# Gated linear attention ahead of two expert layers: units of 256 tokens, with neighbouring decays multiplied before the transposes

## The chip, the cores and the metric

One core of a Trainium2 chip runs the whole program as one launch. The metric is device microseconds of an execution, as the median of the runs shown; times come from the hardware profiler's records of one more execution.

## The reference

The program is a gated linear attention followed by two feed-forward layers, in float32. Only the first part is touched by the change.

```
q,k,v,f_logit: [4 batches, 8 heads, 768 tokens, 48]
f = 1/(1+exp(-f_logit))
for t in range(768):                    # per batch and head
    state = f[t][:,None]*state + outer(k[t], v[t])      # 48 x 48
    y[t] = q[t] @ state
x = y as [3072 tokens, 384]
# then: 8 experts of 384 tokens each, filled in the order of the gate's logits:
#       relu(x @ w1[e]) @ w2[e]       (384 -> 1024 -> 384)
# then: h = x @ w_in; (h*clip(h+3,0,6)/6) @ w_out       (384 -> 2048 -> 384)
```

## The kernel before

`attention` works through the 3,072 tokens in chunks of C=128 (24 chunks, index j). Inside a chunk the recurrence is a masked matrix product; from chunk to chunk a state of 48 x 48 a head is carried. The decays enter as running products: q is multiplied by P, the product of the decays from the chunk's start up to its token (prefix), k by S, the running product taken from the chunk's end and started from the reciprocal of the whole (suffix).

What a chunk needs of q, k and f is prepared in units of U=384 tokens (three chunks, 8 units, index u). Raw f, k and q of a unit are loaded with three consecutive tokens a partition (runs of 3·48 floats, 576 bytes; `load`, L60), v with one token a partition (192 bytes, L64). `reorder` (L66 to L70) moves one of the three tokens at a time into a padded layout: tanh for f on ScalarE (`pmf`), a copy for k on ScalarE (`pmk`), a copy for q on GpSimd (`pmq`). `tgroup` (L72) handles one pair of heads p and one of f, k, q: three transposes (L85) into a PSUM tile of the pool pT (five banks), so that channels are on partitions and 384 tokens lie along the row; for f an ACT pass makes f=0.5·tanh+0.5 (`ff`, L89; two buffers), VectorE runs the prefix scan (L97), takes the product at each chunk's end, held above 2^-60 (L99), its reciprocal (L100), and the suffix scan (L95). For k and q, VectorE multiplies the transposed tile by S (`kh`, L102) or P (`qt`, L109). Unit 0 goes through the same ahead of the loop, by halves of the heads, with q's multiply on GpSimd (L107). The order of the twelve groups of a unit is the list ORD; `group` puts the VectorE operations of one group behind the transposes of the next.

The loop over j (L271 to L305) does, in each turn, in this order: group; `l_mm` for chunk j-1 (L218: output projected into place and gate logits; eviction `y` on ScalarE, store to x_dram); group; `ya_mm` (L142: q times state of chunk j; L136: the 128 x 128 scores of chunk j+1 into banks pA0 and pA1); their evictions `am` on ScalarE (L168) with masking on GpSimd (L169); `y_mm` (L193: masked scores times v; eviction `yt`); `kv_mm` (L204: turned keys times v, into bank pA0) whose result updates the state on VectorE and GpSimd (L209, L211, L212); group; `kt_mm` (L176: keys of chunk j+1 turned back, eviction `kt`); group. Three turns prepare one unit ahead.

In the gaps runs `prep`, a list of steps that fetches float64 weights w_in (twelve blocks of 512 KB) and half of w_out (eight of 384 KB) and converts them on VectorE, ScalarE and GpSimd (L922 to L959, L719, L720). PREP says at which groups a step is taken. All loads and stores are issued by SP in program order. PSUM has eight banks: five for pT, pA0, pA1, and one (`pC`) which holds the constant operand of the prefix scan and the floor 2^-60.

After the loop come the routing of tokens to experts and 8 experts with both feed-forward layers.

Of the kernel before, what the change touches and what calls it, by code (L numbers as in the profile page):

```python
# [14 lines left out]
C=128; U=384; NP=4; NU=B*S//U; NCH=B*S//C  # L15
PMIN=2.0**-60; PB=5

def attention(tc, q,k,v,f,wg, x_dram, lg, ident, pmin, ranges, prep, setup, spin):
    nc=tc.nc
    ctx=ExitStack()  # L20
    with ctx:
# [21 lines left out]
        for i in range(2):  # L43
            t=cs.tile([128,3,H,64],F32,name=f"v{i}"); nc.gpsimd.memset(t[:,:,:,D:],0.0); VP.append(t)
# [4 lines left out]
        for i in range(2):  # L49
            s=cs.tile([128,NP,64],F32,name=f"St{i}"); nc.vector.memset(s[:,:,D:],0.0); St.append(s)  # L50
        FF=[]
        for i in range(2):
            t=cs.tile([128,U+1],F32,name=f"ff{i}"); nc.vector.memset(t[:,U:],1.0); FF.append(t)
        raw={}
        def load(u,nm,h0=0,h1=H):
            b,hf=divmod(u,2)
            if nm!='v':
                src={'f':f,'k':k,'q':q}[nm]
                t=ld.tile([128,H,3*D],F32,name=nm+"r",bufs=1) if h0==0 else raw[nm,u]
                nc.sync.dma_start(t[:,h0:h1],bass.AP(tensor=src.tensor,offset=src.offset+b*H*S*D+h0*S*D+hf*U*D,ap=[[3*D,128],[S*D,h1-h0],[1,3*D]]))  # L60
# [5 lines left out]
        def reorder(u,nm,r,h0=0,h1=H):  # L66
            x=raw[nm,u].rearrange("p h (r d) -> p h r d",d=D)[:,h0:h1,r]; o=perm[nm].rearrange("p r a s d -> p (a s) r d")[:,h0:h1,r,:48]
            if nm=='f': nc.scalar.activation(o,x,AF.Tanh,scale=0.5)
            elif nm=='k': nc.scalar.copy(o,x)
            else: nc.gpsimd.tensor_scalar(o,x,1.0,0.0,op0=OP.mult,op1=OP.add)  # L70
        KH={};QT={};PC={};PP={};SS={};SF={}
        def tgroup(u,p,nm):  # L72
            if p==0 and nm=='f':
                PC[u]=pmin[:,u]
            if p==0 and nm=='k':
                KH[u]=KHB[u%2]
            if p==0 and nm=='q':
                t=wk.tile([128,NP,U],F32,name="qt"); QT[u]=t
            if u==0:
                n=ORD.index((p,nm))%4  # L80
                pt=ps.tile([128,C*3],F32,name=("pT","pA0","pT","pA1")[n],bufs=PB if n%2==0 else 1).rearrange("p (c r) -> p c r",r=3)
            else: pt=ps.tile([128,C,3],F32,name="pT",bufs=PB)
            x=perm[nm]
            for r in range(3):
                nc.tensor.transpose(pt[:,:,r],x[:,r,p].rearrange("p a d -> p (a d)"),ident)  # L85
            pf=pt.rearrange("p c r -> p (c r)")
            if nm=='f':
                ff=FF[p%2]
                nc.scalar.activation(ff[:,:U],pf,AF.Identity,bias=half[:,0:1],scale=0.5)  # L89
                if p%2==0: PP[u,p//2]=wk.tile([128,2,U],F32,name="P")  # L90
                P2=PP[u,p//2]; P=P2[:,p%2]; pp=slice(p-1,p+1)
                V=nc.vector; ends=lambda t: t.rearrange("p a (c t) -> p a c t",t=C)[:,:,:,C-1]
                def suffix():
                    SS[u,p]=wk.tile([128,U],F32,name="S",bufs=3)
                    V.tensor_tensor_scan(SS[u,p][:,::-1],ff[:,1:U+1][:,::-1],m1[:,p%2,::-1],1.0,op0=OP.mult,op1=OP.max)  # L95
                SF[u,p]=suffix
                ops=[lambda: V.tensor_tensor_scan(P,m0,ff[:,:U],1.0,op0=OP.max,op1=OP.mult)]  # L97
                if p%2==0: return ops,[]
                return (ops+[lambda: V.tensor_tensor(out=PC[u][:,pp],in0=ends(P2),in1=least,op=OP.max)],  # L99
                        [lambda: V.reciprocal(ends(m1),PC[u][:,pp]),SF[u,p-1]])  # L100
            elif nm=='k':
                return [lambda: nc.vector.tensor_mul(KH[u][:,p],pf,SS[u,p])],[]  # L102
            else:
                if u==0:
                    t=wk.tile([128,2,NP,C],F32,name="am").rearrange("p s a c -> p (s a c)")[:,:U]
                    nc.scalar.copy(t,pf)
                    nc.gpsimd.tensor_tensor(out=QT[u][:,p],in0=t,in1=PP[u,p//2][:,p%2],op=OP.mult)  # L107
                def whole_q():
                    if u>0: nc.vector.tensor_mul(QT[u][:,p],pf,PP[u,p//2][:,p%2])  # L109
                return [whole_q],([] if p%2 else [SF[u,p+1]])  # L110
        prev=([],[]); rest=[]; late=[]
        def group(new,fill=None,flush=False):

            nonlocal prev,rest
            a=list(rest); b=list(prev[0]); ops=[]
            while a or b:
                if a: ops.append(a.pop(0))
                if b: ops.append(b.pop(0))
            for i,op in enumerate(ops):
                op()  # L120
                if i==0 and fill: fill(); fill=None
            while late: late.pop(0)()
            if fill: fill()
            rest=prev[1]; prev=new
            if flush:
                for op in prev[0]: op()
                prev=([],prev[1])
        AM={};KT={};pA={}
        def a_mm(j):
            u,c=divmod(j,3)  # L130
            pA[j]=[]
            for s in range(2):
                t=ps.tile([128,NP,C],F32,name=f"pA{s}"); pA[j].append(t)
            def quarter(p,s,h):
                r=slice(64*s,64*s+64); k=c*C+64*h
                nc.tensor.matmul(pA[j][s][64*h:64*h+64,p],KH[u][r,p,k:k+64],QT[u][r,p,c*C:(c+1)*C],start=True,stop=True)  # L136
            return quarter
        def s_mm(j):
            u,c=divmod(j,3)
# [30 lines left out]
        def kt_mm(j):  # L170
            u,c=divmod(j,3)
# [25 lines left out]
        def kv_mm(j):  # L197
            u,c=divmod(j,3); first=j%6==0
# [27 lines left out]
        ORD=[(0,'f'),(1,'f'),(0,'q'),(0,'k'),(2,'f'),(3,'f'),(1,'q'),(1,'k'),(2,'q'),(2,'k'),(3,'q'),(3,'k')]  # L226
# [5 lines left out]
        def reorder0(h,nms='fkq'):  # L232
            for nm in nms:
                for r in range(3): reorder(0,nm,r,h,h+4)
        reorder0(0,'fq')
        for nm in 'fkq': load(1,nm)
        WARM=(4,1,8,0); RF,RK=2,4
# [5 lines left out]
        for i,(p,nm) in enumerate(ORD):  # L243
            if i==RF: reorder0(0,'k'); reorder0(4,'f')
            if i==RK: reorder0(4,'q')
            if i==RK+2: reorder0(4,'k')
            group(tgroup(0,p,nm),flush=(p,nm)==ORD[-1])
            warm(WARM[3] if i<2 else WARM[1] if i<11 else WARM[2])
        later=[]
        def refill(u,nm):  # L250
            if u<NU:
                if nm in 'fk':
                    for r in range(3): byact.append(lambda r=r: reorder(u,nm,r))
                    if u+1<NU: byact.append(lambda: later.append(lambda: load(u+1,nm)))
                    return
                for r in range(3): reorder(u,nm,r)
                if u+1<NU: later.append(lambda: load(u+1,nm))
        byact=[]
        def one():

            if byact: byact.pop(0)()
            if len(byact)==1: byact.pop(0)()
        refill(1,'f')
        while byact: one()
        for nm in 'kq': refill(1,nm)
        one(); one()
# [3 lines left out]
        PREP=((0,2),(0,),(0,1,2))  # L270
        for j in range(-1,NCH+1):  # L271
            tu,ti=divmod(j+1,3)
            tu+=1
            g=[(tu,)+x for x in ORD[4*ti:4*ti+4]] if tu<NU else [None]*4
            if j>=0 and j%3==0 and j//3+1<NU: load(j//3+1,'v')
            def take(j,i):
                for _ in range(int(i in PREP[ti]) if j<20 else 2): next(prep,None)
            def tg(i):
# [4 lines left out]
            if ti!=1: one()  # L283
# [853 lines left out]
```

## Time and profile before

| | |
|---|---|
| median of three runs | 845.35 us (845.16 to 845.64) |
| the profiled execution | 842.33 us |
| its span, first to last instruction | 840.5 us |
| busy: TensorE, VectorE, ScalarE, GpSimd | 796.7, 560.4, 366.2, 141.3 us |
| mean granted TensorE clock | 0.988 of full speed |

Attention takes about the first 170 us of the span, the experts the rest from about 195 us on. The busy shares over the whole span are those of the experts, which keep TensorE full; what the change touches has to be read in the first 170 us alone. PE is TensorE's matmuls, PEld its weight loads, DVE VectorE, ACT ScalarE, POOL GpSimd, SP the engine that issues the transfers.

### The profile page before, as it was taken

Reading aid. Unit: us, or ns where it says so; the run is one execution under the profiler, and the core shown is the slowest. Engines: PE = TensorE matmul, PEld = TensorE weight load, DVE = VectorE, ACT = ScalarE, POOL = GpSimd, SP = SyncE. Lnnn points to the kernel's source line nnn. Section 1 sums busy time; section 2 is a strip of 40 time slices with the busy share of each in tenths; the row PEclk is TensorE's granted clock in tenths of the full one; section 3 lists DMA queues with packets and bytes.
Section 4 is the critical chain, followed back from the end, with each engine's and each line's share of the span. In section 5 each row is a group of like instructions: output and inputs, shape, how many; then the busy total and the mean of one; then the engine's idle time right before and its main releaser. Section 6 shows DMA issues by size and latency. Waiting matters only on the chain.

```text
span 840.5 us, 16833 instructions
## 1 busy us (share of the span) xinstructions
PE 796.7 (95%) x6447; PEld 762.4 (91%) x6447; DVE 560.4 (67%) x1526; ACT 366.2 (44%) x759; POOL 141.3 (17%) x233
## 2 busy tenths in 40 slices
PE   7898999888999999999999999999999999999994
PEld 6777788777989899899999999999999999999994
DVE  7999999778688548745964776666757523642431
ACT  5666776514345325423541454154316423541431
POOL 4665653311001101010100101100300020010001
PEclk9999999969999999999999999999999999999998
DMA  8899994173013112211422232322222321321000
GB/s 222 233 244 236 221 232 128 64 244 97 1 37 114 57 39 76 85 39 57 141 72 94 67 97 91 101 66 86 89 81 85 94 85 57 115 93 45 3 1 33
DMA packets 86554, 84.56 MB, mean 101 GB/s; under 512 B 30272, under 2 KB 74432, under 8 KB 86464
## 3 DMA queue, kind: packets, MB, share of 16 engines
q1 hardware_dynamic: 83392, 73.96, 31.1%
q0 software_dynamic: 3072, 9.44, 3.5%
q8 instruction: 52, 0.85, 0.4%
q14 instruction: 38, 0.31, 0.1%
HBM read 73.94 MB, written 9.44 MB: 99 GB/s over the span
## 4 chain that ended last, share of the span: by engine, by line
PE 64%; DVE 15%; issue 12%; ACT 5%; DMA 2%; POOL 2%; SPq 0%; POOLq 0%; ACTq 0%; DVEq 0%
PE acc L723 9%; PE pF L723 9%; PE acc L725 9%; PE acc L724 9%; PE pF L724 9%; PE pF L725 9%; PE pT L85 2%; DVE ga L866 2%; PE pA L136 1%; PE pT L218 1%; DVE hl L869 1%; PE pT L193 1%; DVE S L95 1%; ACT hh L868 1%; PE pA L204 1%
## 5 line engine op out<-in xcount | busy, mean ns | idle before, releaser
L723 PE MATMUL acc<-wo,hh 128*128 128x384 f32 x384 | 133.6, 348 | 0.0
L866 DVE SCALAR_TENSOR_TENSOR ga<-ga,pF 128x384 f32<-128x384 f32 x128 | 70.8, 553 | 92.4 <-ACT ga L865 91.9
L723 PE MATMUL pF<-xh,wih 128*128 128x384 f32 x384 | 131.0, 341 | 0.0
L724 PE MATMUL pF<-xh,wil 128*128 128x384 f32 x384 | 129.4, 337 | 0.0
L725 PE MATMUL acc<-wo,hh 128*128 128x384 f32 x384 | 129.3, 337 | 0.0
L725 PE MATMUL pF<-xl,wih 128*128 128x384 f32 x384 | 129.3, 337 | 0.0
L724 PE MATMUL acc<-wo,hl 128*128 128x384 f32 x384 | 129.1, 336 | 0.1
L865 ACT ACTIVATE ga<-pF,three 128x384 f32<-128x384 f32 x128 | 74.3, 580 | 96.5 <-PE pF L725 89.8
L868 ACT CAST hh<-ga 128x384 fp32r<-128x384 f32 x128 | 65.8, 514 | 98.1 <-DVE ga L866 97.4
L869 DVE TENSOR_TENSOR hl<-ga,hh 128x384 fp32r<-128x384 f32 x128 | 71.2, 556 | 29.7 <-ACT hh L868 27.7
L900 POOL DMA_INDIRECT out_dram<-ga,q_ids x24 | 24.3, 1014 | 395.6 <-ACT ga L898 392.8
L831 ACT ACTIVATE hh<-pF 128x384 fp32r<-128x384 f32 x64 | 31.5, 492 | 130.9 <-PE pF L725 125.9
L832 DVE SCALAR_TENSOR_TENSOR hl<-pF,hh 128x384 fp32r<-128x384 f32 x64 | 35.5, 555 | 70.3 <-ACT hh L831 69.9
L723 PEld LDWEIGHTS acc<-wo,hh 128*128 128x128 f32 x384 | 72.2, 188 | 1.6 <-ACT ga L865 1.5
L724 PEld LDWEIGHTS acc<-wo,hl 128*128 128x128 f32 x384 | 72.2, 188 | 0.4 <-DVE hl L869 0.4
L724 PEld LDWEIGHTS pF<-xh,wil 128*128 128x128 f32 x384 | 72.2, 188 | 0.0
L723 PEld LDWEIGHTS pF<-xh,wih 128*128 128x128 f32 x384 | 72.1, 188 | 0.0
L725 PEld LDWEIGHTS pF<-xl,wih 128*128 128x128 f32 x384 | 72.1, 188 | 0.0
L725 PEld LDWEIGHTS acc<-wo,hh 128*128 128x128 f32 x384 | 72.0, 188 | 0.0
L723 PE MATMUL pF<-xh,w1h 128*128 128x384 f32 x192 | 66.1, 344 | 0.6 <-ACT xh L801 0.6
L723 PE MATMUL acc<-hh,w2h 128*128 128x384 f32 x192 | 65.9, 343 | 0.0
L725 PE MATMUL acc<-hl,w2h 128*128 128x384 f32 x192 | 64.6, 336 | 0.3 <-DVE hl L832 0.2
(288 smaller groups left out, 1653.1 us busy)
## 6 DMA issues: line engine op xcount, KB each, us to landing
wst<-in_moe_w_dram SPq DMA_DIRECT2D x58, 192.0 KB, 2.4
wst<-in_moe_w_dram SPq DMA_DIRECT2D x42, 256.0 KB, 2.9
pw<-in_moe_w_in_dram SPq DMA_DIRECT2D x12, 512.0 KB, 4.7
wo<-in_moe_w_out_dram SPq DMA_DIRECT2D x16, 384.0 KB, 5.5
pm<-in_moe_w_out_dram SPq DMA_DIRECT2D x32, 192.0 KB, 2.5
pm<-in_moe_w_in_dram SPq DMA_DIRECT2D x30, 192.0 KB, 2.5
v<-in_v_dram SPq DMA_DIRECT2D x24, 192.0 KB, 6.2
x_dram<-y SPq DMA_DIRECT2D x24, 192.0 KB, 4.3
```

Of the source, the lines that this page charges most:

```text
L85: nc.tensor.transpose(pt[:,:,r],x[:,r,p].rearrange("p a d -> p (a d)"),ident)
L95: V.tensor_tensor_scan(SS[u,p][:,::-1],ff[:,1:U+1][:,::-1],m1[:,p%2,::-1],1.0,op0=OP.mult,op1=OP.max)
L723: nc.tensor.matmul(out, ahi, bhi, start=start, stop=False)
L724: nc.tensor.matmul(out, alo, bhi, start=False, stop=False)
L725: nc.tensor.matmul(out, ahi, blo, start=False, stop=stop)
L831: nc.scalar.activation(hh,p,AF.Relu)
L832: s.defer(2,lambda: nc.vector.scalar_tensor_tensor(hl,p,0.0,hh.bitcast(F32),op0=OP.max,op1=OP.subtract))
L865: nc.scalar.activation(a,p,AF.Relu,bias=s.three[:,0:1])
L866: late(f,1,lambda: nc.vector.scalar_tensor_tensor(g,a,6.0,p,op0=OP.min,op1=OP.mult))
L868: late(f,1,lambda: nc.scalar.copy(gh,g))
L869: late(f,3,lambda: nc.vector.tensor_tensor(out=gl,in0=g,in1=gh.bitcast(F32),op=OP.subtract))
L900: st=nc.gpsimd.indirect_dma_start(out=s.out,out_offset=bass.IndirectOffsetOnAxis(ap=ids[:,t:t+1],axis=0),in_=o,in_offset=None)
```

## The change

A unit becomes 256 tokens (two chunks, 12 units) with two consecutive tokens a partition (runs of 2·48 floats, 384 bytes). With neighbours side by side on a partition, f of the even and of the odd token are multiplied ahead of the transpose (`decay`: tanh and 0.5·x+0.5 on ScalarE, the product on VectorE), so that f is transposed and scanned by pairs: 64 pairs of a chunk and one leading place, L=65, two heads' pairs and two chunks in one scan. The decay that a pair's own tokens still need is multiplied into one of the two rows beforehand: k of the even token by f of the odd one (`keys`, VectorE), q of the even token by its f (`queries`, GpSimd); the other row is only copied. After the transposes, `scaled` multiplies two pairs of heads at once, 512 elements: for k the same suffix product for both tokens of a pair, for q the product before the pair and the one after it (an overlapping window of two). q and k now go through VectorE for unit 0 too. The scan's constant of one chunk place shrinks, and the key-value product moves from bank pA0 into pC beside it. The order of the work is written out in two tables, PET (transposes) and OPS (VectorE), by eight slots over two turns of the loop; PREP and the places of the reorders are new.

```diff
-C=128; U=384; NP=4; NU=B*S//U; NCH=B*S//C
+C=128; U=256; G=C//2; NP=4; NU=B*S//U; NCH=B*S//C
...
+        L=G+1; W2=4*L
+        held=ps.tile([128,512],F32,name="pC"); m0=held[:,:W2]; KV=held[:,W2:W2+NP*D].rearrange("p (a d) -> p a d",a=NP)
...
-                nc.sync.dma_start(t[:,h0:h1],bass.AP(tensor=src.tensor,offset=...,ap=[[3*D,128],[S*D,h1-h0],[1,3*D]]))
+                nc.sync.dma_start(t[:,h0:h1],bass.AP(tensor=src.tensor,offset=...,ap=[[2*D,128],[S*D,h1-h0],[1,2*D]]))
...
+        def decay(u,i,h0=0,h1=H):
+            x=ft[:,:,h0:h1]
+            if i==0: nc.scalar.activation(x,view(u,'f')[:,:,h0:h1],AF.Tanh,scale=0.5)
+            elif i==1: nc.scalar.activation(x,x,AF.Identity,bias=half[:,0:1],scale=0.5)
+            else: nc.vector.tensor_mul(perm['f'].rearrange("p a s d -> p (a s) d")[:,h0:h1,:48],ft[:,0,h0:h1],ft[:,1,h0:h1])
+        def keys(u,i,h0=0,h1=H):
+            x=view(u,'k')[:,:,h0:h1]
+            if i==0: nc.vector.tensor_mul(home('k',0)[:,h0:h1],x[:,0],ft[:,1,h0:h1])
+            else: nc.scalar.copy(home('k',1)[:,h0:h1],x[:,1])
+        def queries(u,i,h0=0,h1=H):
+            x=view(u,'q')[:,:,h0:h1]
+            if i==0: nc.gpsimd.tensor_tensor(out=home('q',0)[:,h0:h1],in0=x[:,0],in1=ft[:,0,h0:h1],op=OP.mult)
+            else: nc.gpsimd.tensor_scalar(home('q',1)[:,h0:h1],x[:,1],1.0,0.0,op0=OP.mult,op1=OP.add)
+        def decays(u,pairs):
+            pt=ps.tile([128,512],F32,name="pT",bufs=PB).rearrange("p (a c g) -> p a c g",a=NP,c=2)
+            for p in pairs: nc.tensor.transpose(pt[:,p]...,perm['f'][:,p]...,ident)
+            for h in sorted({p//2 for p in pairs}):
+                ff=FF[h][:,:W2].rearrange("p (a c g) -> p a c g",a=2,c=2)
+                nc.scalar.copy(ff[:,:,:,1:],pt[:,2*h:2*h+2])
+        def prefix(u,h):
...
+            V.tensor_tensor_scan(x...,FF[h][:,:W2],m0,1.0,op0=OP.mult,op1=OP.max)
+        def ends(u,h):
+            PC[u]=pmin[:,u]; c=PC[u][:,2*h:2*h+2]
+            V.tensor_tensor(out=c,in0=PX[u,h][:,:,:,G],in1=least,op=OP.max)
+            V.reciprocal(m1[h]...[:,:,:,G],c)
+        def suffix(u,h):
...
+            V.tensor_tensor_scan(x[:,::-1],FF[h][:,1:W2+1][:,::-1],m1[h][:,::-1],0.0,op0=OP.mult,op1=OP.max)
+        def turned(u,nm,h):
...
+                for r in range(2):
+                    nc.tensor.transpose(pt[:,a,:,r],perm[nm][:,r,2*h+a].rearrange("p s d -> p (s d)"),ident)
+        def scaled(u,nm,h):
...
+            if nm=='k': i1=x[:,:,1:][:,:,:,None].to_broadcast([128,4,G,2])
             else:
+                i1=x[:,:,0:G]; i1=bass.AP(tensor=i1.tensor,offset=i1.offset,ap=list(i1.ap)+[[1,2]])
+            V.tensor_tensor(out=out,in0=i0,in1=i1,op=OP.mult)
+        PET={0:lambda u: decays(u,range(NP)),2:lambda u: turned(u,'q',0),3:lambda u: turned(u,'k',0),4:lambda u: turned(u,'q',1),6:lambda u: turned(u,'k',1)}
+        OPS={1:((prefix,0),(ends,0)),2:((prefix,1),(suffix,0)),3:((scaled,'q',0),(ends,1)),4:((scaled,'k',0),(suffix,1)),5:((scaled,'q',1),),7:((scaled,'k',1),)}
...
-            pk=ps.tile([128,512],F32,name="pA0")[:,:NP*D].rearrange("p (a d) -> p a d",a=NP)
+            pk=KV
...
-        PREP=((0,2),(0,),(0,1,2))
+        PREP=((2,0,1,0),(0,1,1,0)); END=(1,0)
         for j in range(-1,NCH+1):
-            tu,ti=divmod(j+1,3)
+            tu,ti=divmod(j+1,2)
...
+            if ti==1: refill(tu+1,'f',2)
             if 0<=j<NCH: y_mm(j,1)
             if j>=0: kv_mm(j)
-            if ti==1: refill(tu+1,'f')
+            if ti==1: refill(tu+1,'q',0)
             tg(2)
-            if ti==1: one()
+            if ti==0: refill(tu+1,'f',0)
+            if ti==1: refill(tu+1,'q',1)
             if j+1<NCH: kt_mm(j+1)
-            if ti==2: refill(tu+1,'q')
             tg(3)
-            if ti==1: one()
-            if ti==2: refill(tu+1,'k'); one(); one()
+            if ti==0: refill(tu+1,'f',1)
+            if ti==1:
+                for i in range(2): refill(tu+1,'k',i)
```

## Rows read from the trace of the kernel before

**Rows 1.** Stages: length, busy time and count of five engines, clock, DMA share, GB/s.
```profile
20.00:140.00 120.00, 107.70 (x1839) 94.61 (x1828) 113.84 (x219) 84.18 (x186) 69.23 (x125) 1.00 0.89 227
140.00:170.00 30.00, 27.00 (x493) 23.94 (x493) 23.67 (x67) 15.54 (x36) 10.12 (x16) 1.00 0.18 59
```

**Rows 2.** Chain of waits, 20 to 140 us: shares by line; two pieces (start, length).
```profile
by line: PE pT L85 14.0%; PE pA L136 8.7%; PE pT L218 8.0%; DVE S L95 7.5%; PE pT L193 6.7%; issue 6.5%; PE pA L204 6.3%; DMA qr<-in_q_dram 5.8%; PE pT L142 5.5%; ACT am L168 4.0%; DVE qt L109 3.6%; ACT ff L89 3.6%; DVE kh L102 3.5%; DVE pm
...
46.35 0.49 ACT am L168
...
46.88 0.67 PE pA L204 x16
```

**Rows 3.** Waits, 20 to 140 us: total, times, longest.
```profile
PE pA L204 <- ACT am L168: 8.4, 12, 2.0
...
ACT ff L89 <- DVE S L95: 5.2, 7, 1.2
```

**Rows 4.** Groups of VectorE, 0 to 170 us: busy us, mean ns, idle before.
```profile
L95 DVE TENSOR_TENSOR_SCAN S<-ff,m 128x384 f32<-128x384 f32 x32 | 31.6, 992 | 0.1
L97 DVE TENSOR_TENSOR_SCAN P<-pC,ff 128x384 f32<-128x384 f32 x32 | 30.0, 946 | 7.0 <-ACT ff L89 6.5
L102 DVE TENSOR_TENSOR kh<-pT,S 128x384 f32<-128x384 f32 x28 | 15.2, 544 | 0.2 <-PE pT L85 0.2
L109 DVE TENSOR_TENSOR qt<-pT,P 128x384 f32<-128x384 f32 x28 | 15.2, 542 | 0.4 <-PE pT L85 0.2
...
L211 DVE TENSOR_TENSOR St<-St,pA 128x192 f32<-128x192 f32 x16 | 5.5, 344 | 2.6 <-PE pA L204 2.4
...
L959 DVE TENSOR_TENSOR wo<-pm,wo 128x384 fp32r<-128x384 f32 x8 | 4.4, 551 | 2.4 <-ACT wo L957 2.3
...
L100 DVE RECIPROCAL m<-pmin 128x6 f32<-128x6 f32 x16 | 3.0, 187 | 0.2
L99 DVE TENSOR_TENSOR pmin<-P,pC 128x6 f32<-128x6 f32 x16 | 2.5, 158 | 0.3
...
L209 DVE TENSOR_TENSOR St<-pA,pmin 128x192 f32<-128x192 f32 x4 | 1.4, 353 | 0.1
```

**Rows 5.** The same view over the whole span: a short scan of the routing.
```profile
L648 DVE TENSOR_TENSOR_SCAN q_inc<-r_zero,q_mem 128x24 f32<-128x24 f32 x8 | 1.7, 207 | 0.2
```

**Rows 6.** Timeline, 18 to 20 us: start, length, operation.
```profile
18.28 0.69 PEld L85 LDWEIGHTS pT<-ident,pmf 128*128 128x128 f32 x6
```

**Rows 7.** Groups of ScalarE and GpSimd, 0 to 170 us.
```profile
L89 ACT ACTIVATE ff<-pT,half 128x384 f32<-128x384 f32 x30 | 17.5, 583 | 9.6 <-DVE S L95 5.2 <-PE pT L85 2.1 <-PE pT L193 1.9
L194 ACT COPY yt<-pT 128x256 f32<-128x256 f32 x38 | 12.7, 399 | 0.0
...
L68 ACT ACTIVATE pmf<-fr 128x384 f32<-128x384 f32 x21 | 10.9, 535 | 1.3 <-DMA fr<-in_f_logit_dram 1.3
...
L68 ACT ACTIVATE pmf<-fr 128x192 f32<-128x192 f32 x6 | 1.7, 352 | 2.8 <-DMA fr<-in_f_logit_dram 2.8
...
L70 POOL TENSOR_SCALAR pmq<-qr 128x384 f32<-128x384 f32 x21 | 13.8, 681 | 2.9 <-DMA qr<-in_q_dram 2.9
...
L107 POOL TENSOR_TENSOR qt<-am,P 128x384 f32<-128x384 f32 x4 | 5.6, 1424 | 3.2 <-DVE pmin L99 2.0 <-ACT am L106 1.2
```

**Rows 8.** Transfers at 22.5 to 23.5 and at 104.8 to 106.5 us, with queue share.
```profile
DMA packets 547, 0.33 MB, mean 331 GB/s; under 512 B 3, under 2 KB 542, under 8 KB 547
...
DMA packets 1465, 0.28 MB, mean 164 GB/s; under 512 B 1465, under 2 KB 1465, under 8 KB 1465
...
q1 hardware_dynamic: 1465, 0.28, 153.8%
```

**Rows 9.** The start: a piece of the chain, and the first scores product.
```profile
13.94 6.95 DMA qr<-in_q_dram
...
19.13 1.10 PE L136 MATMUL pA<-qt,kh 64*64 64x128 f32 x32
```

**Rows 10.** The suffix scans in 20 to 140 us.
```profile
L95 DVE TENSOR_TENSOR_SCAN S<-ff,m 128x384 f32<-128x384 f32 x26 | 25.1, 967 | 0.0
```

More of the change, by code (lines that the diff above doesn't have):

```diff
@@ L61, in load @@
             else:
                 t=VP[u%2]
-                for c in range(3):
-                    nc.sync.dma_start(t[:,c,:,:D],bass.AP(tensor=v.tensor,offset=v.offset+b*H*S*D+(hf*U+c*C)*D,ap=[[D,C],[S*D,H],[1,D]]))
+                for c in range(2):
+                    nc.sync.dma_start(t[:,c,:,:D],bass.AP(tensor=v.tensor,offset=v.offset+b*H*S*D+(o+c*C)*D,ap=[[D,C],[S*D,H],[1,D]]))
             raw[nm,u]=t
[L66 to L102, printed above, removed]
-            else:
[L104 to L121, printed above, removed]
+        view=lambda u,nm: raw[nm,u].rearrange("p h (r d) -> p r h d",d=D)
+        home=lambda nm,r: perm[nm][:,r].rearrange("p a s d -> p (a s) d")[:,:,:48]
@@ new lines, in attention @@
+        PT={}
+        def turned(u,nm,h):
+            pt=ps.tile([128,512],F32,name="pT",bufs=PB).rearrange("p (a g r) -> p a g r",a=2,r=2)
+            for a in range(2):
+                for r in range(2):
+                    nc.tensor.transpose(pt[:,a,:,r],perm[nm][:,r,2*h+a].rearrange("p s d -> p (s d)"),ident)
+            PT[u,nm,h]=pt
+        def scaled(u,nm,h):
+            if nm=='k': o=KH[u]=KHB[u%2]
+            elif h==0: o=QT[u]=wk.tile([128,NP,U],F32,name="qt")
+            else: o=QT[u]
+            pt=PT.pop((u,nm,h))
+            x=(SX if nm=='k' else PX)[u,h]
+            x=x.rearrange("p a c g -> p (a c) g")
+            i0=pt.rearrange("p a (c g) r -> p (a c) g r",c=2); out=o[:,2*h:2*h+2].rearrange("p a (c g r) -> p (a c) g r",c=2,r=2)
+            if nm=='k': i1=x[:,:,1:][:,:,:,None].to_broadcast([128,4,G,2])
+            else:
+                i1=x[:,:,0:G]; i1=bass.AP(tensor=i1.tensor,offset=i1.offset,ap=list(i1.ap)+[[1,2]])
+            V.tensor_tensor(out=out,in0=i0,in1=i1,op=OP.mult)
@@ new lines, in attention, with slot @@
+        late=[]
+        PET={0:lambda u: decays(u,range(NP)),2:lambda u: turned(u,'q',0),3:lambda u: turned(u,'k',0),4:lambda u: turned(u,'q',1),6:lambda u: turned(u,'k',1)}
+        OPS={1:((prefix,0),(ends,0)),2:((prefix,1),(suffix,0)),3:((scaled,'q',0),(ends,1)),4:((scaled,'k',0),(suffix,1)),5:((scaled,'q',1),),7:((scaled,'k',1),)}
+        def slot(u,n,fill=None):
+            if u<NU and n in PET: PET[n](u)
+            for f,*a in OPS.get(n,()) if u<NU else ():
+                f(u,*a)
+                if fill: fill(); fill=None
@@ L122, in group @@
             while late: late.pop(0)()
             if fill: fill()
[L124 to L127, printed above, removed]
         AM={};KT={};pA={}
         def a_mm(j):
-            u,c=divmod(j,3)
+            u,c=divmod(j,2)
             pA[j]=[]
@@ L138, in s_mm @@
         def s_mm(j):
-            u,c=divmod(j,3)
+            u,c=divmod(j,2)
             def state(p,s):
@@ L180, in y_mm @@
         def y_mm(j,part):
-            u,c=divmod(j,3); first=j%6==0
+            u,c=divmod(j,2); first=j%6==0
             vr=raw['v',u]; last=j==NCH-1
@@ L231, in attention @@
             for o in range(2): nc.sync.dma_start(SW[64*s:64*s+48,o::2,2*D:],wg.rearrange("(p s d) e -> s d p e",p=NP,s=2)[s^o][:,o::2])
[L232 to L237, printed above, removed]
+        WARM=(4,1,8)
         def warm(n):
@@ L242, in attention, with refill @@
         warm(WARM[0])
[L243 to L248, printed above, removed]
+        for h in range(2):
+            hh=(4*h,4*h+4)
+            for i in range(3): decay(0,i,*hh)
+            for i in range(2): queries(0,i,*hh)
+            decays(0,(2*h,2*h+1))
+            for i in range(2): keys(0,i,*hh)
+            prefix(0,h); ends(0,h)
+            warm(WARM[1])
+            turned(0,'q',h); suffix(0,h); scaled(0,'q',h)
+            turned(0,'k',h); scaled(0,'k',h)
+            warm(WARM[1+h])
+        for nm in 'fqk': load(1,nm)
         later=[]
-        def refill(u,nm):
+        def refill(u,nm,i):
             if u<NU:
[L252 to L266, printed above, removed]
+                {'f':decay,'k':keys,'q':queries}[nm](u,i)
+                if u+1<NU and i==(0 if nm=='f' else 1): later.append(lambda: load(u+1,nm))
+        for i in range(3): refill(1,'f',i)
+        for i in range(2): refill(1,'q',i)
+        for i in range(2): refill(1,'k',i)
         next(prep)
@@ L269, in attention, with take, tg @@
         constants,early=setup()
-        PREP=((0,2),(0,),(0,1,2))
+        PREP=((2,0,1,0),(0,1,1,0)); END=(1,0)
         for j in range(-1,NCH+1):
-            tu,ti=divmod(j+1,3)
+            tu,ti=divmod(j+1,2)
             tu+=1
[L274 to L278, printed above, removed]
-                group(tgroup(*g[i]) if g[i] is not None else ([],[]),(lambda: take(j,i)) if j>=0 else None,(ti,i)==(2,3))
+            if j>=0 and j%2==0 and j//2+1<NU: load(j//2+1,'v')
+            def take(i):
+                for _ in range(PREP[ti][i] if j<20 else 2): next(prep,None)
+            def tg(i): slot(tu,4*ti+i,(lambda: take(i)) if j>=0 else None)
             if j==NCH: spin(lambda: ps.tile([128,384],F32,name="pT",bufs=PB),TAIL[0])
@@ L304, in attention @@
             if j in (17,22,24): next(early)
-            if 0<=j<10 or 14<=j<20: next(prep,None)
+            if j<20:
+                for _ in range(END[ti] if j>=0 else 0): next(prep,None)
         for _ in prep: pass
```

50 lines of the change are left out of this document (30 added, 20 removed).

## The prediction

> **What bounds the kernel now.** I read the table of stages first [rows 1]. In the stretch 20 to 140 us the loop over chunks runs at its full load: VectorE is busy 113.8 of 120 us, TensorE 107.7, ScalarE 84.2, GpSimd 69.2, and the DMA share is 0.89 at 227 GB/s. In 140 to 170 us the loop runs out (VectorE 23.7 of 30 us), and after 170 us come routing and the experts, which the change does not touch; they start when attention ends, so I take each microsecond of attention as a microsecond of the total. VectorE looks like the bound, but the chain of waits over that stretch [rows 2] names PE lines ahead of its lines: the transposes (L85) carry 14.0%, the suffix scans (L95) 7.5%, and two ScalarE copies, the eviction of the scores (am, L168) and of the decays (ff, L89), 4.0% and 3.6%. The reader is to see two engines near full that take turns. One turn of theirs is shown in the two pieces there: the last am copy ends and at once TensorE's key-value product (L204) starts, because it is put into the bank that this copy must empty. The waits [rows 3] price it: PE stood 8.4 us for am, and the ff copy stood 5.2 us for a suffix scan to give its buffer back.
>
> **The scans.** Now 32 prefix and 32 suffix scans of 384 elements take 30.0 and 31.6 us [rows 4]. After, 12 units have two of each over 2·2·65=260 elements, 48 in all. A scan of 24 elements took 0.207 us [rows 5] and one of 384 takes 0.946: 2.05 ns an element, so 0.691 for 260, 33.2 us in all: 28.4 saved. Bounds: in proportion to length (30.7 us) and at the old price each (45.4 us).
>
> **The multiplies of q and k.** Now 60 on VectorE (28 of each and unit 0's four for k; unit 0's four for q run on GpSimd), 15.2 us for each 28 [rows 4], so 32.6 us for 60. After, 48 of 512 elements. From PSUM, 192 elements took 0.344 and 384 took 0.544 us: 1.04 ns an element, 0.68 for 512, 32.6 us: even. What no row shows is an operand that is read twice or in overlapping pairs; the nearest, the row with a broadcast operand, is 0.353 against 0.344. I take no penalty; the far end is the scan's 2.05 ns an element, 1.21 us each, 25 us more.
>
> **New on VectorE.** f·f and k·f ahead of the transposes: two of 384 elements a unit, 0.551 each by the row of a 384-element two-operand operation out of SBUF (L959 [rows 4]), 13.2 us. The ends and reciprocals go from 16 to 24 pairs at 0.158+0.187: 8.3 for 5.5 us, 2.8 more. The memsets stand ahead of the first f and change little; zero. VectorE's balance is −28.4+13.2+2.8=−12.4 us.
>
> **TensorE.** 288 transposes become 240: f needs one per pair of tokens instead of one per token, q and k stay at 96 each. Six loads of such a group take 0.69 us [rows 6], 0.12 each, so 5.8 us less. The key-value product gets a place of its own beside the scan's constants, so its wait for am goes; what is late next is the following chunk's scores product, which needs that bank anyway.
>
> **ScalarE and GpSimd.** Tanh goes from 192 to 384 elements by 0.183 us [rows 7], so a unit's two tokens a partition, 768 elements, take about 0.90; the second pass over them, now out of PSUM, another 0.90: 21.6 us for 12 units where tanh takes 12.6 now. The eviction of the decays shrinks from 32 of 0.583 to 24 of 256 elements, 0.399 by the row of that size: 9.6 for 18.7 us; half of the key copies go too. The sum is below the present one. Of the order: tanh stands ahead of the copy of the turned keys (kt), on which the next chunk's key-value product waits; half a chunk lies between. GpSimd's multiply of q takes 1.42 us by its four rows and its copy 0.681, 25 us for the present 22. It stands in its queue ahead of the state's update, which the next state product asks for after most of a chunk. Neither engine is full, so I put both at nothing; if the cover went, the multiply would cost 1.4 us a unit.
>
> **Transfers.** q, k and f come in runs of 384 bytes instead of 576; 36,864 runs for 24,576. The stretches where one kind runs alone [rows 8] give 547 packets of 576 bytes in 1 us on 16 engines (29.2 ns each) and 1,465 of 192 bytes in 1.7 us (18.6 ns). Midway lies 23.9 ns, 257 GB/s, so 55.1 us for the 44.9 now: 10.2 more. The ends are the price of a 192-byte packet (no more time at all, 42.8 us) and the rate of 192-byte packets, 164 GB/s (86.3 us, 41.4 more). The queue's own work now: v 28.6 us, the three streams 44.9, x (4.7 MB) and the weights (9.4 MB) at 331 GB/s 14.3 and 28.5, 116 us. Of its 33 MB, 27.2 fall into 20 to 140 us, 82%: 95 of 120 us. (The share of 0.89 is larger because packets overlap on an engine: the full stretch of small packets reads 153.8% [rows 8].) After: 95+8.4=103 us in some 113; hidden, but with a tenth to spare. SP issues in one order, so a late q load would hold back the key load and v behind it, and behind a late q stands GpSimd's masking of the scores.
>
> The Trainium skill, DMA: Bandwidth & Descriptors, section Specifications, asks for at least 512 bytes a transfer for line rate and says that below it the engine reads, modifies and writes. The trace agrees for 192 bytes (164 against 331 GB/s); for 384 no row shows it. By the rule's harsh reading the three streams would run at the 192-byte rate, the 41.4 us above. That is the far end of rival (3) below.
>
> **The start.** The first scores product begins at 19.13 us, and the chain there goes through the load of unit 1's q, which lands at 20.9 [rows 9]. Until then the queue moves 3,456 KB in runs of 576 bytes and 576 KB of v: 10.7+3.6=14.3 us of transfer and 5.8 of latency and gaps. After: 2,304 KB at 257 GB/s and 384 KB of v, 9.2+2.4, so 2.7 us earlier. But unit 0 then covers two chunks instead of three; the third chunk's share (3.4 us of VectorE, ten transposes) moves into the loop and costs about 1.7 there. Net −1.0. Bounds: −3.5 (the extra share hidden in the idle time of the start), and +1.5, because the loop's first round asks for tanh of unit 2, whose f is loaded behind unit 1's k and two weight blocks of 512 KB.
>
> **The sum in the loop**, by the shares of the chain [rows 2] on 120 us. Transposes 16.8 us, a sixth gone: −2.8 (0 to −5.8). Scans: L95 9.0 us, and L97, which the line no longer shows and so has 3.5% or less, taken as 3.6 us; 46% gone: −5.8. The ff copies 4.3 us, half gone: −2.1. am ahead of the key-value product, 4.8 us, of which I take half: −2.4. The 16.0 us that VectorE gains count in the share in which its suffix scans stand on the chain (9.0 of 25.1 us in this stretch [rows 10], 36%): +5.8. Together −7.3, with the start −8.3. Around its span of 840.5 us the profiled execution took 842.33; the median of the runs, 845.35, is 3.0 above it, and I carry the difference over: 837.0 us.
>
> **Rivals.** (1) Only TensorE's work counts and VectorE's free time turns into waiting: −2.8−1.0, 841.5 us. For it: PE leads the chain. Against: VectorE idles for 6 us in 120 only. (2) VectorE alone is the bound: −12.4−1.0, and at best the waits of ff and am besides, −4.5: 827 to 832 us. (3) The transfers become the pace, slower than before: the loop wants 95 us plus 82% of the extra. It exceeds 113 us when a 384-byte packet takes over 29 ns (212 GB/s) and has eaten the whole gain at about 33 ns. At 164 GB/s: 95+34=129 us for 120, +9, and the start +2.5 instead of −2.7, with its +1.7: 858.5 us. For it: a tenth to spare is little for a queue that moves in bursts. Against: a 576-byte packet takes no more than 29 ns. (4) The pairwise operand runs at the scan's rate: VectorE is at +12.6 instead of −12.4. By the chain's share that is +9.0 on −8.3, 846 us; as the only bound 857. Against: the broadcast row.
>
> **Chances.** The likeliest course 0.52, own range 832 to 841; (1) 0.20; (2) 0.08; (3) 0.14; (4) 0.06. The range takes in most of (2) and the lower half of (3): 829 to 850. A difference within 0.2% (1.7 us) can't be told from none here. Faster by more: nearly all of the first three cases, 0.78; within it 0.07; slower, from (3) and (4), 0.15.
>
> **What would show it.** Right: scans near 0.69 us and multiplies near 0.68; no wait of the key-value product for am; first scores product near 17 us; the loop's end (VectorE's last 512-element multiplies in a chunk, then the experts' weight loads) some 8 us earlier. Wrong: multiplies near 1.2 us; waits of ScalarE or GpSimd for fr and qr in the steady loop; a stretch of 384-byte packets under 212 GB/s; VectorE's busy share falling below nine tenths while PE's rises only by what the shorter stretch gives.

## The result: slower by 0.8%

The changed kernel takes 851.88 us (median of 4 runs, 849.52 to 854.05), the kernel before it 845.25 on the same chip (843.76 to 845.64): a ratio of 1.0081, interval 1.0052 to 1.0111. The forecast of 837.0 us is wrong in sign, and the time lies above the range. The profiled execution took 849.52 us with a span of 847.6.

The stages, columns as in [rows 1], and then three pieces of the loop:

```profile
20.00:140.00 120.00, 98.98 (x1689) 88.33 (x1681) 105.56 (x212) 73.83 (x159) 72.57 (x119) 0.97 0.83 209
140.00:170.00 30.00, 25.54 (x455) 22.67 (x455) 24.16 (x59) 16.77 (x39) 10.37 (x16) 1.00 0.44 113
40.00:50.00 10.00, 8.31 (x144) 7.83 (x148) 5.14 (x14) 5.26 (x10) 5.56 (x11) 0.83 0.87 227
50.00:60.00 10.00, 6.13 (x112) 5.28 (x103) 9.85 (x19) 4.09 (x10) 7.19 (x9) 0.93 0.61 168
60.00:70.00 10.00, 10.00 (x136) 8.95 (x130) 7.53 (x15) 7.33 (x15) 4.08 (x9) 0.90 0.73 191
```

TensorE and VectorE are both less busy than before (98.98 for 107.70 us, 105.56 for 113.84): neither is the bound, they wait. VectorE does 5.14 us of work in one stretch of ten and 9.85 in the next. The clock, 1.00 before, is 0.97, with pieces down to 0.83.

The loop starts earlier, as forecast, and then loses. The first scores product, from the timeline (19.13 us in [rows 9]):

```profile
16.38 1.10 PE L144 MATMUL pA<-qt,kh 64*64 64x128 f32 x32
```

The value product (`y_mm`) of chunk 0 starts at 20.4 us (25.3 before), that of chunk 12 at 107.4 (102.9), that of the last at 173.3 (166.0). Twelve chunks went from 77.6 to 87.0 us.

Four of the waits in 20 to 170 us (total, times, longest):

```profile
...
PE pT L150 <- POOL St L220: 13.8, 7, 3.1
...
POOL St L220 <- DVE St L219: 11.4, 8, 1.9
ACT am L176 <- PE pA L144: 10.3, 6, 3.3
DVE P L97 <- PE pC L212: 9.0, 7, 4.7
```

Before, TensorE's wait for the state's update was 0.4 us in the same stretch, and no scan of VectorE waited for that product; the wait for am (8.4 us in [rows 3]) is gone. One turn of them, from the timeline:

```profile
36.01 0.35 DVE L219 TENSOR_TENSOR St<-St,pC 128x192 f32<-128x192 f32 x1
...
36.26 1.55 POOL L718 TENSOR_TENSOR wil<-pm,wih 128x512 fp32r<-128x512 f32 x1 [3.77 <-ACT wih L717]
...
37.77 1.99 POOL L177 TENSOR_SCALAR_AFFINE_SELECT am<-am 128x512 f32<-128x512 f32 x2
...
39.73 1.43 POOL L84 TENSOR_TENSOR pmq<-qr,ft 128x384 f32<-128x384 f32 x1
...
41.12 0.51 POOL L220 TENSOR_TENSOR St<-St,pmin 128x192 f32<-128x192 f32 x1
...
41.69 0.48 PE L150 MATMUL pT<-qt,St 64*64 64x128 f32 x2 [3.08 <-POOL St L220]
...
41.95 0.42 PE L150 MATMUL pT<-qt,St 64*64 64x128 f32 x2
...
45.60 0.62 PE L212 MATMUL pC<-v,kt 128*64 128x48 f32 x16
...
46.27 0.69 DVE L97 TENSOR_TENSOR_SCAN P<-ff,pC 128x260 f32<-128x260 f32 x1 [4.71 <-PE pC L212]
```

VectorE's half of the state's update (L219) ends at 36.36 us, but GpSimd's half (L220) begins at 41.12: a weight conversion (L718), the masking of the scores (L177) and the multiply of q (L84) are ahead of it in GpSimd's queue. TensorE stands 3.08 us for the update, its matmuls then take 0.42 instead of 0.28 us, the key-value product is late, and the second prefix scan, whose constant lies in that product's bank, keeps VectorE idle for 4.71 us.

The same turn in the kernel before, from its timeline:

```profile
34.53 0.34 DVE L211 TENSOR_TENSOR St<-St,pA 128x192 f32<-128x192 f32 x1
35.20 0.51 POOL L212 TENSOR_TENSOR St<-St,pmin 128x192 f32<-128x192 f32 x1
36.67 0.33 PE L142 MATMUL pT<-qt,St 64*64 64x128 f32 x2
...
36.83 0.28 PE L142 MATMUL pT<-qt,St 64*64 64x128 f32 x2
```

There the second half follows the first after 0.3 us, and the update is ready 1.0 us before the state product that needs it. Over 20 to 140 us it was ready 0.6 to 1.6 us ahead, in chunks of some 6.5 us.

The groups of VectorE and GpSimd (0 to 190 us) that answer to [rows 4] and [rows 7]:

```profile
L105 DVE TENSOR_TENSOR_SCAN S<-ff,m 128x260 f32<-128x260 f32 x24 | 19.7, 819 | 0.1
L97 DVE TENSOR_TENSOR_SCAN P<-ff,pC 128x260 f32<-128x260 f32 x24 | 16.5, 688 | 10.9 <-PE pC L212 9.0 <-ACT ff L93 1.9
L124 DVE TENSOR_TENSOR kh<-pT,S 128x512 f32<-128x512 f32 x24 | 16.3, 680 | 0.0
...
L80 DVE TENSOR_TENSOR pmk<-kr,ft 128x384 f32<-128x384 f32 x11 | 10.4, 948 | 0.5 <-DMA kr<-in_k_dram 0.5
...
L77 DVE TENSOR_TENSOR pmf<-ft 128x384 f32<-128x384 f32 x11 | 7.1, 643 | 1.6 <-ACT ft L76 1.6
```

```profile
L84 POOL TENSOR_TENSOR pmq<-qr,ft 128x384 f32<-128x384 f32 x11 | 14.1, 1280 | 5.9 <-ACT ft L76 5.9
L220 POOL TENSOR_TENSOR St<-St,pmin 128x192 f32<-128x192 f32 x16 | 9.7, 606 | 11.4 <-DVE St L219 11.4
L85 POOL TENSOR_SCALAR pmq<-qr 128x384 f32<-128x384 f32 x11 | 8.1, 740 | 0.0
```

The operations with an operand in PSUM (L97, L124) run at the forecast 0.69 and 0.68 us. Those with both operands in SBUF do not: the suffix scan takes 0.819 for 0.691, k·f 0.948 and f·f 0.643 for 0.551.

### The profile page after: what moved, and what is told of

Its sections match the earlier page's. It is cut to its first block, busy times and chain, and to the rows that moved or that the text cites. A ratio compares the mean times of both kernels' runs of the same rounds, so it can differ in the third digit from the quotient of the medians.

```text
span 847.6 us, 16704 instructions
## 1 busy us (share of the span) xinstructions
PE 795.2 (94%) x6387; PEld 763.4 (90%) x6387; DVE 556.5 (66%) x1541; ACT 358.2 (42%) x732; POOL 144.2 (17%) x228
## 4 chain that ended last, share of the span: by engine, by line
PE 56%; issue 10%; DVE 8%; ACT 3%; DMA 1%; POOL 1%; POOLq 0%; DVEq 0%; ACTq 0%; SPq 0%
PE pF L721 9%; PE acc L721 9%; PE pF L722 9%; PE pF L723 9%; PE acc L723 9%; PE acc L722 9%; DVE ga L864 2%; DVE hl L867 1%; ACT hh L866 1%; ACT ga L863 1%; DVE w1l L770 1%; PE pF L808 1%; POOL out_dram L898 1%; DMA wst<-in_moe_w_dram 1%; DVE q_ge L499 0%
## 5 line engine op out<-in xcount | busy, mean ns | idle before, releaser
L722 PE MATMUL pF<-xh,w1l 128*128 128x384 f32 x192 | 65.2, 340 | 0.0
```

The lines of the kernel that those rows point to most:

```text
L722: nc.tensor.matmul(out, alo, bhi, start=False, stop=False)
```

## The experiments

Each ran beside the kernel before, on the same chip; all ratios are to that kernel. Four theories: **(A)** GpSimd's work on q delays the state's update; **(B)** the bank shared by the scan's constants and the key-value product stalls VectorE; **(C)** VectorE's operations on two SBUF operands are held up beside GpSimd; **(D)** the lower clock after TensorE's waits costs time of its own. The expectations, written before each run, use other letters: their theory A is the bank, here (B); their B is GpSimd's queue, here (A); their C is the transfers; their D is VectorE held up beside GpSimd and the late update, here (C) and (A).

**GpSimd's multiply of q (A).** First its place in the queue, then its engine:

```diff
-            if ti==1: refill(tu+1,'q',0)
             tg(2)
...
-            if ti==1: refill(tu+1,'q',1)
+            if ti==1:
+                for i in range(2): refill(tu+1,'q',i)
```

> GpSimd's multiply of q is recorded behind the state's update instead of ahead of it; nothing else changes. Theory B: PE's wait for St falls from 13.8 us to under 3, the key-value product comes earlier, so also the wait of the scan on it shrinks: 842 to 847 us. Theory A: PE's wait for St falls but the scan still stands behind the key-value product; 848 to 852 us. Theory C: nothing changes.

849.09 us, ratio 1.0061 (1.0039 to 1.0084): not told apart from the changed kernel, and above the 842 to 847 us that A would have. The update was then queued ahead of q, but began only 1.2 us earlier (39.91 for 41.12 us): weight conversion and masking stand ahead of it too. TensorE's wait fell to 7.9 us, VectorE's stayed (10.0). The value product of chunk 12 began 4.1 us earlier than in the changed kernel (103.3 for 107.4 us), the last one at the same time (173.3 us). The granted clock was 0.83 in 40 to 50 us, 0.83 in 103 to 113 and 0.84 in 141 to 152. By these figures TensorE lost some 5.2 us to the clock, an estimate, so this run does not rule the place in the queue out.

```diff
-            if i==0: nc.gpsimd.tensor_tensor(out=home('q',0)[:,h0:h1],in0=x[:,0],in1=ft[:,0,h0:h1],op=OP.mult)
+            if i==0: nc.vector.tensor_mul(home('q',0)[:,h0:h1],x[:,0],ft[:,0,h0:h1])
```

> The multiply of q's even tokens is done by VectorE instead of GpSimd (0.55 us more on VectorE a unit, 6 us in all; GpSimd loses 13 us). Theory B: the state's update no longer stands behind it, PE's wait for St falls under 3 us; and VectorE's k multiply (0.948 us instead of 0.55) and suffix scan (mean 0.819 instead of 0.69) get their undisturbed lengths if GpSimd's multiply beside them stretched them, 7 us less on VectorE. 841 to 847 us. Theory A: L97's wait for pC stays, 849 us or more.

843.31 us, ratio 1.0003 (0.9993 to 1.0013): this one line takes the whole loss back, though VectorE gets 6.4 us more to do in these eleven multiplies. The waits there:

```profile
PE pT L150 <- POOL St L220: 7.0, 8, 1.3
...
DVE P L97 <- PE pC L212: 3.4, 7, 1.0
```

The longest waits went from 3.1 and 4.7 us to 1.3 and 1.0, and the clock in 20 to 140 us is 1.00. TensorE's wait did not fall under 3 us as expected: conversion and masking are still ahead of the update. Nor did VectorE's operations get their undisturbed lengths: the suffix scan stays at 819 ns, k·f goes from 948 to 832 and f·f from 643 to 580, 2.0 us in all against the 6.4 added. So the move gave the time back through the waits and the clock, hardly through C.

**The shared bank (B).** The constants into SBUF, and this together with the later q:

```diff
-        held=ps.tile([128,512],F32,name="pC"); m0=held[:,:W2]; KV=held[:,W2:W2+NP*D]...
+        held=cs.tile([128,512],F32,name="hold"); m0=held[:,:W2]; KV=ps.tile([128,512],F32,name="pC")[:,:NP*D]...
```

> The scan's constants (m0 and the floor) lie in a tile of their own in SBUF; the key-value product keeps bank pC to itself. Theory A (the shared tile: the second prefix scan of a unit stands behind the same chunk's key-value product, 9.0 us of waits in 7 places): the wait of L97 for pC is gone and 5 to 9 us come back, 843 to 847 us. Theory B (GpSimd's queue: the state's update stands behind the multiply of q, PE waits 13.8 us for St): little changes, the wait of L97 moves elsewhere, 849 to 853 us. Theory C (transfers in runs of 384 bytes): nothing changes.

> Both edits together. If both mechanisms are real and feed each other, this run gets what the balance of work promised: 835 to 840 us, faster than the kernel before. If either one alone was the cause, it equals that one's run within 2 us.

851.63 us, 1.0096 (1.0075 to 1.0118), and 852.83 us, 1.0113 (1.0089 to 1.0138): no gain. The scan no longer waits for the bank, but it is now an operation on two SBUF operands, at 921 for 688 ns, 5.6 us more for 24:

```profile
L97 DVE TENSOR_TENSOR_SCAN P<-ff,hold 128x260 f32<-128x260 f32 x24 | 22.1, 921 | 2.0 <-ACT ff L93 1.9
```

So this edit put another loss in place of B's and can't price B; it showed that the scan is slower with its constant in SBUF. A cleaner test keeps the constants in PSUM and puts both prefix scans ahead of the key-value product:

```diff
-        OPS={1:((prefix,0),(ends,0)),2:((prefix,1),(suffix,0)),3:((scaled,'q',0),(ends,1)),...
+        OPS={1:((prefix,0),(ends,0),(prefix,1),(ends,1)),2:((suffix,0),),3:((scaled,'q',0),),...
```

> The second prefix scan and its ends are recorded one slot earlier, ahead of the chunk's key-value product, so that the shared bank no longer makes VectorE wait; all tiles stay where they are, so no operand moves between PSUM and SBUF. Theory A (the wait on the shared bank, 9.0 us): the wait of L97 for pC goes and 4 to 8 us come back, 844 to 848 us. Theory D (VectorE's operations with both operands in SBUF are stretched beside GpSimd, and the state's update is late on GpSimd): the wait turns into others, 849 to 853 us.

> The scans ahead as in the run before, and q's multiply on VectorE. Theory A and the GpSimd theory together: 837 to 841 us, below the kernel before. If the wait on the bank was only a consequence of PE being late, it equals the run with q on VectorE, 843 us.

Alone 845.84 us, 1.003 (1.0015 to 1.0044); with the q multiply on VectorE 841.5 us, 0.9973 (0.996 to 0.9985), just above the 837 to 841 us expected. The scan's wait is gone, at its old price:

```profile
L97 DVE TENSOR_TENSOR_SCAN P<-ff,pC 128x260 f32<-128x260 f32 x24 | 16.2, 676 | 1.7 <-ACT ff L93 1.7
```

Without the multiply moved, VectorE now stands 7.5 us (0.8 before this edit) for the same product at the state's sum (L219) instead. Still, B is a real part, about 0.5% alone and 0.3% on top of the moved multiply. The other way out is to put the product back into bank pA0, as before:

```diff
-            pk=KV
+            pk=ps.tile([128,512],F32,name="pA0")[:,:NP*D].rearrange("p (a d) -> p a d",a=NP)
```

> The changed kernel with one part undone: the key-value product goes into the first scores bank again, as in the kernel before, and not beside the scan's constants. If moving it is a part of the loss: the second prefix scan no longer waits for the key-value product (9.0 us in the changed kernel), in its place TensorE waits for the am copies (8.4 us in the kernel before), and since a scan that stands in VectorE's full queue costs more than that, the whole is 846 to 849 us, still above the kernel before because GpSimd's q multiply still stands ahead of the state's update. If the shared bank only shows a delay that the state product carries anyway: 851 to 853 us.

847.73 us, 1.0063 (1.0047 to 1.0079): not told apart from the changed kernel. TensorE waits for am again (14.8 us), and VectorE 11.6 us for the product: one wait for the other.

**GpSimd without q.** The fastest version so far (e6_ahead_q_vector), with q's other half copied on ScalarE:

```diff
-            else: nc.gpsimd.tensor_scalar(home('q',1)[:,h0:h1],x[:,1],1.0,0.0,op0=OP.mult,op1=OP.add)
+            else: nc.scalar.copy(home('q',1)[:,h0:h1],x[:,1])
```

> As the run before, and q's odd tokens are copied by ScalarE instead of GpSimd (8.6 us less on GpSimd, some 6 us more on ScalarE, which is busy 51 of 80 us). Theory D (GpSimd's own time decides: the state's update comes late and VectorE is stretched): 3 to 5 us faster than the run before it. If ScalarE's queue is the tighter one (scores' eviction behind the copy): the same or 2 us slower.

838.85 us, 0.9948 (0.9928 to 0.9969): faster than both kernels (its interval overlaps that of the version before it, e6_ahead_q_vector, so the 3 to 5 us expected over that version are not shown). In 20 to 100 us VectorE is now all but full, 78.42 of 80 us, at full clock:

```profile
20.00:100.00 80.00, 68.97 (x1217) 61.25 (x1210) 78.42 (x153) 54.99 (x118) 44.37 (x68) 1.00 0.93 231
```

With the product put back into pA0 in this version:

> The fastest version so far (both prefix scans ahead, nothing of q on GpSimd, 838.85 us) with the key-value product back in the first scores bank. If the move to the constants' bank is worth something once no scan waits on it: slower than that version, 841 to 844 us, with a wait of the key-value product for am of some 6 to 8 us. If the wait for am is hidden there: 838 to 840 us.

843.81 us, 1.0009 (0.9991 to 1.0026), with 15.4 us of waiting for am. The move to the constants' bank, worth nothing in the changed kernel, is worth 0.6% (1.0009 against 0.9948) where no scan stands behind it. Part of that may be the clock: it was 0.83 in 60 to 70 us here and 1.00 there.

**VectorE beside GpSimd (C).** Two measurements of single operations:

> Leaves out the whole program; it times four VectorE operations alone and beside three kinds of GpSimd work: a scan of 260 elements with both operands in SBUF and with one in PSUM, a product of 384 elements out of SBUF and of 512 with one operand in PSUM. Theory D: with one operand in PSUM nothing changes (0.69 and 0.68 us); with both in SBUF the operation takes 0.1 to 0.5 us longer while GpSimd works, most beside its two-operand product. If the long means in the kernel were waits and not stretched operations, all four keep their lengths.

The order of this one's operations was not kept as written, so its pairings can't be read by name. The second fixes the order by data dependences:

> Leaves out the whole program and measures single operations: eight of each of VectorE's four forms (scan of 260 with both operands in SBUF, multiply of 384 with both in SBUF, scan of 260 with one operand in PSUM, multiply of 512 with one in PSUM), each beside nothing and beside eight GpSimd operations of one kind (the q multiply of 384, the masking of 512, the copy of 384), in an order that data dependences fix, which the measurement before it did not. If GpSimd's reads hold up VectorE's second SBUF operand: the forms with a PSUM operand stay at 0.68 us in every pairing; the scan of two SBUF operands goes from 0.67 to 1.3 to 1.5 us beside the multiply and less beside the operations with one operand. If it is GpSimd's work as such: the forms with a PSUM operand stretch too.

Groups of VectorE: beside nothing (L36, L51, L66), the multiply (L40, L55, L70), the masking (L44, L59) and the copy (L48, L63); then GpSimd's multiply beside the scan of two SBUF operands (L39) and the one with a PSUM operand (L69):

```profile
L40 DVE TENSOR_TENSOR_SCAN o<-a,b 128x260 f32<-128x260 f32 x8 | 9.9, 1232 | 0.5 <-POOL go L33 0.3
L55 DVE TENSOR_TENSOR o<-a,b 128x384 f32<-128x384 f32 x8 | 9.2, 1148 | 0.5 <-POOL go L33 0.3
L44 DVE TENSOR_TENSOR_SCAN o<-a,b 128x260 f32<-128x260 f32 x8 | 7.3, 916 | 0.5 <-POOL go L33 0.3
L59 DVE TENSOR_TENSOR o<-a,b 128x384 f32<-128x384 f32 x8 | 6.7, 832 | 0.5 <-POOL go L33 0.3
L48 DVE TENSOR_TENSOR_SCAN o<-a,b 128x260 f32<-128x260 f32 x8 | 6.4, 803 | 0.5 <-POOL go L33 0.3
L63 DVE TENSOR_TENSOR o<-a,b 128x384 f32<-128x384 f32 x8 | 5.7, 718 | 0.5 <-POOL go L33 0.3
L36 DVE TENSOR_TENSOR_SCAN o<-a,b 128x260 f32<-128x260 f32 x8 | 5.6, 699 | 0.5 <-POOL go L33 0.3
L66 DVE TENSOR_TENSOR_SCAN o<-a,bank 128x260 f32<-128x260 f32 x8 | 5.6, 695 | 0.5 <-POOL go L33 0.3
L70 DVE TENSOR_TENSOR_SCAN o<-a,bank 128x260 f32<-128x260 f32 x8 | 5.6, 695 | 0.5 <-POOL go L33 0.3
...
L51 DVE TENSOR_TENSOR o<-a,b 128x384 f32<-128x384 f32 x8 | 4.5, 559 | 0.5 <-POOL go L33 0.3
```

```profile
L39 POOL TENSOR_TENSOR go<-ga,gb 128x384 f32<-128x384 f32 x8 | 10.3, 1286 | 0.6
...
L69 POOL TENSOR_TENSOR go<-ga,gb 128x384 f32<-128x384 f32 x8 | 7.9, 993 | 0.6
```

With both operands in SBUF the scan goes from 699 to 1232 ns beside the multiply, and GpSimd's multiply from 993 to 1286: both lose. With an operand in PSUM the scan stays at 695 in every pairing, the 512-element multiply at 691. The Trainium skill, SBUF — State Buffer, section Who interferes with whom, says that a VectorE instruction with two SBUF inputs contends with a GpSimd instruction that reads SBUF; these rows agree. What C costs the kernel no run shows: the suffix scan is at 819 ns with q's multiply on VectorE and at 832 with nothing of q on GpSimd, where masking and weight conversion are still done.

**The clock (D).** Unused matmuls where TensorE had stood for the state's update:

```diff
+            if j in (3,5): warm(22)
             ya_mm(j)
```

> The changed kernel with 22 matmuls of 128 columns added, whose result nothing uses, ahead of the state product of chunks 3 and 5, where TensorE waited 3.08 and 3.07 us for GpSimd's state update (they end about when that wait does). Nothing else is changed, so the wait, the late scan and VectorE's stretched operations stay. If the lower granted clock after such a wait is a cause of its own: the stretch 40 to 70 us shows a clock near 1.00 instead of 0.83 to 0.93, its scores and state products take 0.28 us a pair again instead of 0.42, and the whole falls by 2 to 4 us, to 848 to 850 us. If the clock only goes along with the waits, which set the time: 851 to 853 us, whatever the clock reads.

855.36 us, 1.0148 (1.0126 to 1.017). It could not tell: each matmul is two instructions, and the filling lasted 5.10 us each time, some 1.8 us beyond the waits. With `warm(11)`:

> The changed kernel with 11 unused matmuls, two instructions each, ahead of the state product of chunks 3 and 5, so that they end about when GpSimd's state update does (22 of them ended 1.8 us too late). All waits and stretched operations stay. If the lower clock after the waits is a cause of its own: clock 1.00 in 40 to 70 us, the value product of chunks 3 and 5 about 1.3 us earlier each than in the changed kernel, the whole 848 to 850 us. If the time gained there only moves into the next wait: clock 1.00 there and the whole 851 to 853 us, with later stretches slower or longer waits further on.

851.96 us, 1.0112 (1.0095 to 1.0129). The clock was 1.00 in 30 to 70 us, and the value product of chunk 7 began at 68.3 us for 71.6; but the waits before chunks 9 and 11 were now 3.07 us each, the clock in 70 to 140 us read 0.94, and the lead was gone: 851 to 853 us was expected if the time gained only moves into the next wait. With these filled too, `j in (3,5,9,11)`:

> The changed kernel with 11 unused matmuls, two instructions each, ahead of the state product of chunks 3, 5, 9 and 11, the four that waited longest when only the first two were filled. If the lower clock carries a part of the loss: clock near 1.00 over the whole of 20 to 140 us, the value product of chunk 11 at 96 to 99 us instead of 102.5, the whole 845 to 849 us. If the time gained always moves into the next wait: 851 to 853 us, with the waits before later chunks longer.

847.33 us, 1.0047 (1.0033 to 1.0061), and the clock is 1.00 throughout:

```profile
20.00:140.00 120.00, 109.09 (x1819) 98.75 (x1818) 106.52 (x217) 75.99 (x165) 74.91 (x122) 1.00 0.88 214
```

Matmuls that compute nothing make the kernel faster, by 0.65% from two filled waits to four (1.0112 to 1.0047, intervals apart). That supports D: the waits cost more than their length. It does not show D as a part of this change's loss: against the changed kernel (1.0081) two filled waits gained nothing, and four gained 0.34% with intervals that overlap. How large D can be there is an estimate: the clocks of 0.83, 0.93 and 0.90 in the three stretches of 10 us above come to 3.4 us of TensorE's time, of 12.2 us that the loop lost. The value product of chunk 11 began at 100.6 us, not at the 96 to 99 expected: more than half of the loss is there at full clock too.

## Why the prediction was wrong

**The step that failed** is "Neither engine is full, so I put both at nothing". GpSimd's multiply of q was seen to stand ahead of the state's update, "which the next state product asks for after most of a chunk", and priced at 1.4 us a unit if that cover went. The cover was not there. The trace of before shows the update ready 0.6 to 1.6 us ahead of the state product, not most of a chunk, and in the changed kernel weight conversion and masking stand ahead of the update besides q's multiply (1.28 us). In the four turns of 20 to 110 us with the multiply in the queue, GpSimd's half of the update began 3.3 to 4.8 us after VectorE's half had ended, and TensorE stood 2.4 to 3.1 us for it. (The 11.4 us that GpSimd stood for VectorE at L220 fall in the other turns, where TensorE stood under 1 us.) TensorE's wait, 13.8 us, is near the price that was named (12 units by 1.4 are 17 us) and then left out; 7.0 of it remain with the multiply on VectorE, but the loss of time is gone. No rival held it: what would have been slower, the transfers and the pairwise operand of rivals (3) and (4), is not what happened.

**What is late next after the moved key-value product** was named wrongly too: not the next scores product but the second prefix scan, ordered behind it in the bank that they share (9.0 us).

**VectorE's balance** was mis-sized: the groups of the changed work sum to 95.5 us for 99.5, −4.0 instead of −12.4. The suffix scans are 3.1 us above the forecast, f·f and k·f 18.9 us for 13.2, both as C has it; the rest of the difference is small. [rows 4] held a hint: the suffix scan with two SBUF operands at 992 ns, the prefix scan of the same length with one in PSUM at 946.

**The sum by shares of the chain** counted what work leaves the path and had no term for what TensorE's idle time does to its clock.

**Right:** prefix scans (0.688 for 0.691 us) and the 512-element multiplies (0.68 and 0.67 for 0.68), which removes rival (4); the am wait gone; the transfers faster than assumed, as the row of a stretch with 384-byte packets alone shows (16 engines over 784 packets in 1 us are 20.4 ns each, for 23.9 assumed), which removes rival (3):

```profile
DMA packets 784, 0.30 MB, mean 296 GB/s; under 512 B 784, under 2 KB 784, under 8 KB 784
```

The rule of the Trainium skill on 512 bytes (DMA: Bandwidth & Descriptors, Specifications), read harshly, is not borne out at 384 bytes. The first scores product came 2.75 us earlier (2.7 forecast for the start's transfers), chunk 0's value product 4.9. In the loop, from chunk 0's value product to the last one's, the time went from 140.7 to 152.9 us: +12.2 where the sum had −7.3; the last one is 7.2 us late, as is the end of the span (7.1). With the two failed steps undone (GpSimd free of q, both prefix scans ahead) the change does pay: 838.85 us for 843.38 on that chip.

**What stays open.** That q's multiply on GpSimd costs the whole loss is shown by moving it. How the loss divides between the waits (A, with B behind them) and the clock (D) is not: e4_q_on_vector takes both back at once. What C costs in time stays open too; VectorE's two-operand work with one operand moved to PSUM was not tried. Nor was the new place of the weight steps (PREP): in the turn shown, GpSimd stood 3.77 us for a weight block from ScalarE and converted it for 1.55 us ahead of masking and update, and TensorE still waited 7.0 us in all with q's multiply gone.

## What to carry to other kernels

An engine with free time is no cover by itself: for each operation put on it, ask what stands behind it in its queue and which full engine waits for that, read from the trace before how long that result now lies ready, and carry the price that you worked out for the lost cover as a rival with a chance. Before work moves between PSUM and SBUF or onto GpSimd, see which VectorE operations read two SBUF operands while GpSimd runs. And when a full TensorE begins to wait, look at its granted clock behind each wait.

## What the runs showed of the hardware that was not expected

- Of the four VectorE forms measured, VectorE and GpSimd slow each other in the two where VectorE reads both operands from SBUF, and not in the two with one in PSUM: 699 to 1232 ns for the scan and 993 to 1286 ns for GpSimd's multiply; for the scan beside the masking 916 and beside the copy 803.
- Around a wait of 3.08 us of TensorE, in 40 to 50 us, the granted clock was 0.83 on average, part of the stretch at the lower of its levels (1.2 instead of 2.4 GHz), and the state's matmuls behind it took 0.42 instead of 0.28 us a pair; with such waits filled the clock was 1.00.
- Packets of 384 bytes moved at 296 GB/s, between 331 at 576 and 164 at 192 bytes [rows 8].
